# Mode products with the spectrum as the stationary operand and 512 weight columns moving

## Chip, cores, metric

One core of one Trainium2 chip. The metric is device microseconds (us) of one execution. "Before" and "after" are the kernel before and after the change. Medians stand with their ranges. With one core there is no second die to compare; the profiled runs and those in the ratios were judged fast. Times of different kernels are compared inside the same batch of rounds on the same chip. A trace is one profiled execution; its span is some 1.8 us shorter than the timed run, so traces are compared with traces.

## What is computed

Windowed attention (batch 8, 8 heads, 576 positions, head size 64), whose output `x` (8 x 576 x 512) goes into a spectral layer:

```python
X  = np.fft.rfft(x, axis=1)                       # along the sequence
Xr, Xi = X.real[:, :64], X.imag[:, :64]           # 64 modes are kept
Yr = einsum('bmd,mde->bme', Xr, w_r) - einsum('bmd,mde->bme', Xi, w_i)
Yi = einsum('bmd,mde->bme', Xr, w_i) + einsum('bmd,mde->bme', Xi, w_r)
y  = np.fft.irfft(Y, n=576, axis=1)               # Y is zero above mode 64
u  = x + y
return u + np.maximum(u @ w_ch, 0)
```

The weights `w_r` and `w_i` have 64 modes of 512 x 512 each. They are the bulk of what is read. Mode 0 has no imaginary part, so there are 127 products of one weight matrix with 16 rows (8 batches, real and imaginary).

## The kernel before

`XQ` holds the spectrum with contraction on the partitions: for each of four chunks `c` of the 512 channels, for each batch, three rows (-Xi, Xr, Xi) of 64 modes. A product of one weight is 16 small matmuls: a 128 x 128 block of the weight is loaded as the stationary operand and 16 columns of the spectrum move.

```python
def mode(m, between=lambda: None):
    wr, wi = wtiles.pop((m, 0)), wtiles.pop((m, 1), None)
    if m % MG == 0:
        psy = ps_y.tile([128, MG, NC, 2 * B], FP32, name="psy")
    for im, w in enumerate((wr, wi) if m else (wr,)):
        for e in range(NC):
            for c in range(NC):
                nc.tensor.matmul(out=psy[:, m % MG, e, :], lhsT=w[:, c, 128 * e:128 * e + 128],
                                 rhs=XQ[:, c, :, 1 - im:3 - im, m], ...)
        if im == 0:
            between()                 # other PE work: a turned spectrum
        refill_w(m, im)               # this weight's buffer is free: issue the next load into it
    if m % MG == MG - 1 or m == ME - 1:
        keep_y(m)                     # two copies from PSUM into YT
```

Weights come in through one queue, 512 KB a load, issued by POOL when a buffer comes free (`refill_w`):

```python
def load_w(i, pool, tag, wt=None):
    ...
    src = moe_w_i if im else moe_w_r
    nc.gpsimd.dma_start(out=wt, in_=src[m].rearrange("(p c) e -> p c e", c=NC))
```

The last four modes (60 to 63) have products of their own into `psl`, which the change leaves in their old form. Between them PE runs a filler, `idle`, whose results nothing reads:

```python
def idle(wide, n):
    ...                                # 'wide' matmuls of 512 columns, then
    for _ in range(10 * n):
        nc.tensor.matmul(out=psd[:, 0:48], lhsT=ident_bf, rhs=view(x_sb, 0, [[1, 48]]), ...)

for m in range(ME + 2, NM):            # modes 62 and 63
    for im in range(2):
        idle(1, 2)
        last(m, im)
idle(0, 2)
```

The softmax here doesn't subtract the row's maximum and nothing guards it: scores larger than these inputs give would overflow.

## Time and profile before

| | before |
|---|---|
| median of 3 runs | 428.31 us (428.12 to 428.38) |
| span of the trace | 426.7 us |
| instructions | 11631 |
| weight products | 127 x 16 matmuls, each with its weight load |

### The profile page before, as it was taken

What the parts mean: (1) busy time and instruction counts of PE and PEld (TensorE: products, weight loads), DVE (VectorE), ACT (ScalarE), POOL (GpSimd) and SP (SyncE); (2) the same over time, 40 slices, a digit from 0 to 9 for tenths busy, and PEclk for the clock granted to TensorE, in tenths of its full rate; (3) what the DMA queues carried; (4) which work ended last, traced back from release to release, by engine and by line L of the source; (5) the groups of instructions that cost most, each with busy time, mean ns of one, the idle gap of its engine ahead of it and who ended that gap; (6) DMA issues with size and microseconds to landing.
All of it is one profiled execution on the core that took longest, in us unless ns stands there. A gap on an engine that the chain in (4) does not pass through costs nothing.

```text
span 426.7 us, 11631 instructions
## 1 busy us (share of the span) xinstructions
PE 320.8 (75%) x5179; PEld 229.7 (54%) x5190; DVE 178.0 (42%) x375; ACT 165.0 (39%) x292; POOL 89.2 (21%) x171
## 2 busy tenths in 40 slices
PE   6989998999989865322497787887457685498993
PEld 5655765666665665321376666655244452265781
DVE  5566765766673200306333432221113432240994
ACT  4585766866773121001032322222113331130992
POOL 7231231331021321211121121121211122200000
PEclk9999999999995855555588998888558967589997
DMA  7999999999999999999999999999999999994598
GB/s 141 212 213 212 213 212 214 212 214 212 214 213 215 214 214 260 214 214 214 213 214 214 214 213 214 214 213 214 213 214 213 214 214 213 214 212 81 202 392 311
DMA packets 28657, 92.16 MB, mean 216 GB/s; under 512 B 2832, under 2 KB 3088, under 8 KB 28608
## 3 DMA queue, kind: packets, MB, share of 16 engines
q0 software_dynamic: 25344, 81.80, 96.2%
q1 hardware_dynamic: 3120, 9.50, 5.8%
q8 instruction: 40, 0.66, 0.6%
q10 hardware_dynamic: 144, 0.13, 0.1%
q14 instruction: 9, 0.07, 0.0%
HBM read 162.53 MB, written 9.44 MB: 403 GB/s over the span
## 4 chain that ended last, share of the span: by engine, by line
DMA 49%; PE 36%; DVE 8%; issue 4%; ACT 2%; POOL 1%; DVEq 0%; POOLq 0%
DMA wt<-in_moe_w_i_dram 22%; DMA wt<-in_moe_w_r_dram 18%; DMA wy<-in_moe_w_r_dram 9%; PE pso L316 7%; PE pst L218 6%; PE pso L870 4%; PE psv L235 3%; PE psy L563 3%; DVE x_sb L324 3%; PE pss L372 3%; PE pss L272 2%; PE psx L338 2%; PE pss L291 2%; DVE vT L59 2%; PE psz L596 1%
## 5 line engine op out<-in xcount | busy, mean ns | idle before, releaser
L563 PE MATMUL psy<-XQ,wt 128*128 128x16 bf16 x1616 | 61.3, 191 | 73.7 <-DMA wt<-in_moe_w_i_dram 34.7
L563 PEld LDWEIGHTS <-wt 128*128 128x128 bf16 x1616 | 53.0, 103 | 89.6 <-DMA wt<-in_moe_w_i_dram 39.7
L591 DVE CAST xT<-pxt 128x256 fp32r<-128x256 bf16 (+1 forms) x68 | 26.1, 434 | 61.6 <-PE pxt L584 39.7
L598 ACT CAST Z<-psz 128x512 fp32r<-128x512 f32 x36 | 21.1, 586 | 67.5 <-PE psz L596 67.5
L115 POOL DMA_DIRECT2D wt<-in_moe_w_r_dram x54 | 28.9, 536 | 87.3 <-DMA wt<-in_moe_w_r_dram 42.1
L596 PE MATMUL psz<-wch,xT 128*128 128x512 f32 x144 | 46.3, 465 | 0.0
L115 POOL DMA_DIRECT2D wt<-in_moe_w_i_dram x52 | 27.8, 535 | 85.7 <-DMA wt<-in_moe_w_i_dram 49.1
L297 ACT ACTIVATE et<-pss 128x512 bf16<-128x512 f32 x72 | 39.2, 600 | 13.4 <-PE pss L291 13.4
L316 PE MATMUL pso<-vt,et 128*64 128x65 bf16 (+1 forms) x576 | 34.3, 210 | 4.8 <-DVE x_sb L324 4.7
L316 PEld LDWEIGHTS <-et 128*64 128x64 bf16 (+1 forms) x576 | 24.0, 114 | 17.1 <-issue 9.6
L596 PEld LDWEIGHTS psz<-wch,xT 128*128 128x128 f32 x144 | 29.4, 218 | 5.9 <-ACT Z L598 0.3
L324 DVE TENSOR_TENSOR x_sb<-pso,rcp 128x640 bf16<-128x640 f32 x32 | 26.3, 823 | 0.9
L59 DVE CAST x_sb<-psj 128x512 bf16<-128x512 f32 x18 | 12.3, 689 | 26.3 <-PE psj L773 23.4
L870 PE MATMUL pso<-Y,trigI 128*128 128x512 f32 x80 | 23.1, 402 | 0.1
L893 DVE TENSOR_TENSOR ot<-pso,x_sb 128x512 f32<-128x512 f32 x35 | 22.2, 685 | 1.5 <-PE pso L870 1.1
L272 PE MATMUL pss<-band,ident_bf 64*64 64x512 bf16 x136 | 20.7, 414 | 1.5 <-ACT et L297 1.5
L58 ACT CAST YT<-psy 128x256 fp32r<-128x256 f32 x6 | 2.2, 372 | 50.6 <-DVE YT L59 50.6
L59 DVE COPY vT<-pst 128x768 bf16<-128x768 bf16 x16 | 15.3, 958 | 13.0 <-PE pst L218 13.0
L58 ACT CAST x_sb<-psj 128x512 bf16<-128x512 f32 x18 | 10.5, 585 | 25.7 <-PE psj L773 25.7
L59 DVE CAST YT<-psy 128x256 fp32r<-128x256 f32 x6 | 2.5, 425 | 42.9 <-PE psy L563 42.9
L875 ACT ACTIVATE pso<-pso 128x512 f32<-128x512 f32 x36 | 19.2, 596 | 0.0
L870 PEld LDWEIGHTS pso<-Y,trigI 128*128 128x128 f32 x80 | 14.5, 188 | 5.5 <-ACT pso L875 1.7
(160 smaller groups left out, 492.7 us busy)
## 6 DMA issues: line engine op xcount, KB each, us to landing
wt<-in_moe_w_r_dram POOLq DMA_DIRECT2D x54, 512.0 KB, 19.1
wt<-in_moe_w_i_dram POOLq DMA_DIRECT2D x52, 512.0 KB, 19.1
out_dram<-ot SPq DMA_DIRECT2D x15, 512.0 KB, 4.4
rk<-in_k_dram POOLq DMA_DIRECT2D x8, 576.0 KB, 9.8
rq<-in_q_dram POOLq DMA_DIRECT2D x8, 576.0 KB, 13.7
rv<-in_v_dram POOLq DMA_DIRECT2D x8, 576.0 KB, 12.4
wy<-in_moe_w_r_dram POOLq DMA_DIRECT2D x3, 512.0 KB, 17.0
wy<-in_moe_w_i_dram POOLq DMA_DIRECT2D x3, 512.0 KB, 19.1
```

The lines of the kernel that those rows point to most:

```text
L59: return nc.vector.tensor_copy(out=o, in_=i)
L115: nc.gpsimd.dma_start(out=wt, in_=src[m].rearrange("(p c) e -> p c e", c=NC))
L218: nc.tensor.transpose(out=ps[64 * hh:64 * hh + 64, c, :], in_=src[:, hh, (c0 + c) * D:(c0 + c + 1) * D], identity=ident_bf)
L272: nc.tensor.matmul(out=pss[(2 * w + hh) % 3][64 * half:64 * half + 64, :], lhsT=ident_bf[pp, pp], rhs=view(band[pp], 128 * half, [[0, WIN ...
L297: nc.scalar.activation(out=et[:, hh, :], in_=pss[(2 * w + hh) % 3], func=ACT_F.Exp, scale=EX_SCALE)
L316: nc.tensor.matmul(out=pso[po, hh, (i // 2) * VW:(i // 2) * VW + D + 1], lhsT=et[pk, hh, col:col + 64], rhs=vt[pk, 1 - f % 2, 2 * hh + g / ...
L324: nc.vector.tensor_tensor(out=view(x_sb, b * NT * DM + g * D, [[4 * D, 2], [DM, NT], [1, D]]), in0=view(pso, 0, [[512, 2], [VW, NT], [1, D]]),
L563: nc.tensor.matmul(out=psy[:, m % MG, e, :], lhsT=w[:, c, 128 * e:128 * e + 128], rhs=XQ[:, c, :, 1 - im:3 - im, m], start=(m % MG == im + ...
L591: nc.vector.tensor_copy(out=xT[:, :, w * k:w * k + w], in_=view(psts[k], j, [[128, NC], [n, w]] if n > 1 else [[128, NC], [1, 64], [64, 2]]))
L596: nc.tensor.matmul(out=psz, lhsT=xT[:, c, :], rhs=wch[:, c, :], start=(c == 0), stop=(c == NC - 1))
L870: nc.tensor.matmul(out=tps[n], lhsT=trigI[:, tr:tr + 128], rhs=pair_tile(what, bb), start=False, stop=stop and r0 + k == 128, skip_group_c ...
L893: nc.vector.tensor_tensor(out=ot[:, j], in0=ps, in1=x_sb[:, b, t, :], op=ALU.add)
```

## The change

Its intent: let the small operand (32 columns of spectrum) be stationary and the large one (512 weight columns) move, so that one weight costs 4 matmuls and 4 narrow loads in place of 16 and 16. The output then has 16 useful rows and 512 columns, so four modes share one PSUM tile of 128 x 512 as four blocks of 32 rows, and the result has to be turned by transposes every four modes. The spectrum is laid out with modes contiguous so that the 32 stationary columns have one stride.

```diff
-    XQ = xqp.tile([128, NC, B, 3, NM], BF16, name="XQ")
+    XQ = xqp.tile([128, NC, 3, B, NM], BF16, name="XQ")
 ...
-    def keep_y(m):
-        ... (two copies of psy into YT)
+    MQ = 4
+    held = []
+    def keep_y(m, ps):
+        half = [x_sb[:, 4 * (m // MQ % 2) + 1 + 2 * h, NT - 1, :].bitcast(FP32) for h in range(2)]
+        for h in range(2):
+            evac(half[h], ps[:, 256 * h:256 * h + 256], h)
+        def turn_rows():
+            psa = ps_a.tile([128, NC, 128], FP32, name="psa", tag="psa")
+            for e in range(NC):
+                nc.tensor.transpose(out=psa[:, e, :], in_=half[e // 2][:, 128 * (e % 2):128 * (e % 2) + 128], ...)
+            ... (two copies of psa into YT)
+        held.append(turn_rows)
 ...
     def mode(m, between=lambda: None):
-        if m % MG == 0:
-            psy = ps_y.tile([128, MG, NC, 2 * B], FP32, name="psy")
+        if m % MQ == 0:
+            psy = ps_y.tile([128, DM], FP32, name="psy")
+        r0 = 32 * (m % MQ)
         for im, w in enumerate((wr, wi) if m else (wr,)):
-            for e in range(NC):
-                for c in range(NC):
-                    nc.tensor.matmul(out=psy[:, m % MG, e, :], lhsT=w[:, c, 128 * e:128 * e + 128],
-                                     rhs=XQ[:, c, :, 1 - im:3 - im, m], ...)
+            for c in range(NC):
+                k = 32 if c < NC - 1 else 2 * B
+                nc.tensor.matmul(out=psy[r0:r0 + k, :], lhsT=xq(c, m, im, [[NM, k]]), rhs=w[:, c, :], ...)
             if im == 0:
+                while held:
+                    held.pop(0)()
                 between()
 ...
-        for _ in range(10 * n):
-            nc.tensor.matmul(out=psd[:, 0:48], ..., rhs=view(x_sb, 0, [[1, 48]]), ...)
+        for _ in range(5 * n):
+            nc.tensor.matmul(out=psd[:, 0:96], ..., rhs=view(x_sb, 0, [[1, 96]]), ...)
```

Cut: the indexing helper `xq`, the two copies that write the new layout of `XQ`, one copy moved from mode 8 to mode 1, and a last `held` call before the end.

More of the change, by code (lines that the diff above doesn't have):

```diff
@@ L347, in dft_turn @@
                                 identity=ident_bf)
-        BN = B * 3 * NM
-        nc.vector.tensor_copy(out=view(XQ, b * 3 * NM + NM, [[BN, NC], [1, 2 * NM]]), in_=ps.rearrange("p c r m -> p c (r m)"))
-        nc.scalar.mul(out=view(XQ, b * 3 * NM, [[BN, NC], [1, NM]]), in_=ps[:, :, 1, :], mul=-1.0)
+        nc.vector.tensor_copy(out=view(XQ, (B + b) * NM, [[3 * B * NM, NC], [B * NM, 2], [1, NM]]), in_=ps)
+        nc.scalar.mul(out=view(XQ, b * NM, [[3 * B * NM, NC], [1, NM]]), in_=ps[:, :, 1, :], mul=-1.0)
     nw = 0
@@ L540, in refill_w, with xq @@
             nw += 1
-    def rows_of(tile_, n, g, im, m0, nm):
-        return view(tile_, g * 2 * MG + im * nm + m0, [[B * n, NC], [n, B], [1, nm]])
-    def keep_y(m):
-        g = m // MG
-        n = MG if m < M0 + MG else ML
-        dst, k, g = (YT, E0, g) if g < L0 else (YTl, R, g - L0)
-        for ri in range(2):
-            evac(rows_of(dst, k, g, ri, 0, n),
-                 view(psy, ri, [[2 * B, NC], [2, B], [NC * 2 * B, n]]), ri)
+    MQ = 4
[7 more added lines that the diff above has]
+            for e in range(NC):
+                nc.tensor.transpose(out=psa[:, e, :], in_=half[e // 2][:, 128 * (e % 2):128 * (e % 2) + 128],
+                                    identity=ident_r.bitcast(FP32))
+            g = m // MG
+            n = MG if m < M0 + MG else ML
+            dst, k, g = (YT, E0, g) if g < L0 else (YTl, R, g - L0)
+            for ri in range(2):
+                evac(view(dst, g * 2 * MG + ri * n + m % MG - MQ + 1, [[B * k, NC], [k, B], [1, MQ]]),
+                     view(psa, B * ri, [[128, NC], [1, B], [32, MQ]]), ri)
+        held.append(turn_rows)
+    def xq(c, m, im, dims):
+        return view(XQ, (c * 3 + 1 - im) * B * NM + m, dims)
     def mode(m, between=lambda: None):
@@ L557, in mode @@
         wr, wi = wtiles.pop((m, 0)), wtiles.pop((m, 1), None)
-        if m % MG == 0:
-            psy = ps_y.tile([128, MG, NC, 2 * B], FP32, name="psy")
+        if m % MQ == 0:
+            psy = ps_y.tile([128, DM], FP32, name="psy")
+        r0 = 32 * (m % MQ)
         for im, w in enumerate((wr, wi) if m else (wr,)):
-            for e in range(NC):
-                for c in range(NC):
-                    nc.tensor.matmul(out=psy[:, m % MG, e, :], lhsT=w[:, c, 128 * e:128 * e + 128],
-                                     rhs=XQ[:, c, :, 1 - im:3 - im, m], start=(m % MG == im + e + c == 0),
-                                     stop=(im == (m > 0) and c == NC - 1), skip_group_check=True)
+            for c in range(NC):
+                k = 32 if c < NC - 1 else 2 * B
+                nc.tensor.matmul(out=psy[r0:r0 + k, :], lhsT=xq(c, m, im, [[NM, k]]), rhs=w[:, c, :],
+                                 start=(im + c == 0), stop=(im == (m > 0) and c == NC - 1), skip_group_check=True)
             if im == 0:
+                while held:
+                    held.pop(0)()
                 between()
             refill_w(m, im)
-        if m % MG == MG - 1 or m == ME - 1:
-            keep_y(m)
+        if m % MQ == MQ - 1:
+            keep_y(m, psy)
     with ExitStack() as p2a:
@@ L604 @@
             mode(m)
-            if m == 8:
+            if m == 1:
                 for b in range(1, B, 2):
@@ L726, in idle @@
             nc.tensor.matmul(out=psd, lhsT=ident_r.bitcast(FP32), rhs=Z0[:, 0, :].bitcast(FP32), start=True, stop=True)
-        for _ in range(10 * n):
-            nc.tensor.matmul(out=psd[:, 0:48], lhsT=ident_bf, rhs=view(x_sb, 0, [[1, 48]]), start=True, stop=True)
+        for _ in range(5 * n):
+            nc.tensor.matmul(out=psd[:, 0:96], lhsT=ident_bf, rhs=view(x_sb, 0, [[1, 96]]), start=True, stop=True)
     seq = []
@@ L763, in last_mode @@
                                  lhsT=w[:, c, 128 * e:128 * e + 128],
-                                 rhs=XQ[:, c, :, 1 - im:3 - im, m], start=(m == ME and im + c + e == 0),
+                                 rhs=xq(c, m, im, [[NM, B], [B * NM, 2]]), start=(m == ME and im + c + e == 0),
                                  stop=(im == 1 and c == NC - 1), skip_group_check=True)
@@ L803 @@
                 refill_w(m, 1)
+        while held:
+            held.pop(0)()
         NR = 2 * R + RL * (B - 2)
```

## The prediction

> **What bounds the kernel now.** I read the page first, then the chain of waits in order of time, then stretches of the span, then PE's timeline inside them. On the page, the clock, DMA and GB/s rows and the chain:
>
> ```profile
> PEclk9999999999995855555588998888558967589997
> DMA  7999999999999999999999999999999999994598
> GB/s 141 212 213 212 213 212 214 212 214 212 214 213 215 214 214 260 214 214 214 213 214 214 214 213 214 214 213 214 213 214 213 214 214 213 214 212 81 202 392 311
> DMA 49%; PE 36%; DVE 8%; issue 4%; ACT 2%; POOL 1%; DVEq 0%; POOLq 0%
> DMA wt<-in_moe_w_i_dram 22%; DMA wt<-in_moe_w_r_dram 18%; DMA wy<-in_moe_w_r_dram 9%; PE pso L316 7%; PE pst L218 6%; PE pso L870 4%; PE psv L235 3%; PE psy L563 3%; DVE x_sb L324 3%; PE pss L372 3%; PE pss L272 2%; PE psx L338 2%; PE pss L291 2%; DVE vT L59 2%; PE psz L596 1%
> ```
>
> From the second slice to the 36th (about 10 to 385 us) DMA stays at nine tenths and 212 to 214 GB/s, attention or no attention. The program is one stream of loads with compute hung on it. The end of that stream in the chain:
>
> ```profile
> 352.06 17.01 DMA wy<-in_moe_w_r_dram
> 369.60 19.99 DMA wy<-in_moe_w_r_dram
> 389.64 0.63 PE psl L762 x16
> 390.26 0.94 PE psd L726 x2
> 391.21 0.50 PE psd L728 x20
> 391.70 0.49 PE psl L762 x16
> ```
>
> So about 389.6 us is set by the transfers and 37 us of inverse transform follow. A change between 145 and 389 us matters only if it opens a gap in the stream or makes PE late at 389.6. PE there, by stretches (start and end, length, PE, PEld, DVE, ACT, POOL busy, clock, DMA share, GB/s):
>
> ```profile
> 148.58:172.00 23.42, 15.28 (x511) 14.74 (x507) 1.18 (x5) 4.19 (x7) 5.83 (x13) 0.50 1.09 235
> 173.00:210.00 37.00, 9.59 (x240) 8.00 (x240) 12.81 (x54) 2.81 (x11) 7.95 (x15) 0.50 1.06 213
> 211.00:297.00 86.00, 70.92 (x834) 54.32 (x830) 25.55 (x66) 21.48 (x38) 18.52 (x35) 0.88 1.06 214
> 313.00:372.00 59.00, 39.25 (x511) 25.18 (x511) 17.13 (x26) 14.46 (x26) 12.69 (x24) 0.73 1.06 214
> ```
>
> First PE works off the 29 or so weights that lie ready when the spectrum is done (145.6), then waits for each load, then shares its time with the channel products (psz), then with the turned spectra and the spreading of x. The operations to price, in PE's timeline (start, busy):
>
> ```profile
> 180.32 0.67 PE L563 MATMUL psy<-XQ,wt 128*128 128x16 bf16 x16 [1.83 <-DMA wt<-in_moe_w_r_dram]
> 241.06 2.12 PE L596 MATMUL psz<-wch,xT 128*128 128x512 f32 x8
> 322.94 0.62 PE L773 MATMUL psj<-x_sb,ident_bf 128*64 128x512 bf16 x4
> 357.33 1.06 PE L773 MATMUL psj<-x_sb,ident_bf 128*64 128x512 bf16 x4
> ```
>
> Sixteen small products of one weight cost 0.67 us, about 30 ns apart once streaming. Weights come every 2.45 us (PE's starts from 186.09 to 210.62: ten gaps). PE waits 1.83 of that.
>
> [...]eight psz in 2.12 us warm are 264 ns with their weight loads; four psj, two at a time, 0.62 warm and 1.06 cold[...]clock flips lie on a grid of 3.413 us (128.1, 141.8, 148.6, 216.9). [...]the psj pairs (64 output rows each, two column halves, different data) do run concurrently here.[...]
>
> **The change, part by part.**
> (1) Products. 119 weights (modes 0 to 59) go from 16 matmuls and 16 full weight loads to 4 matmuls of 512 columns with 32-column loads: 1428 matmuls and 1428 loads less. Time rises: from 0.48 us streaming to 4 x 0.216 = 0.87 us warm or 4 x 0.427 = 1.71 us cold. The last product of a mode and the first of the next are in different column tiles and may overlap: at best 7/8 of that. So PE gets 119 x 0.4 = 47 us more work warm, 119 x 1.2 = 145 us cold. All beside the stream as long as PE keeps up.
> (2) Turning. Every four modes: two copies of half a bank (0.42 and 0.37 us, the 128x256 rows of the YT copies), four 128x128 transposes (0.4 to 0.63 us, as psa now), two copies of 128 elements a row (0.29 and 0.27). About 1.4 us more latency and 0.5 us of PE for each of 15 groups: 0.06 us a weight.
> (3) Spectrum layout: same copies, other strides: nothing.
> (4) The idle filler: 10 matmuls of 96 columns (43 ns) for 20 of 48 (0.50 us in the chain): about -0.1 us each, twice after the last weight: -0.2 us.
> (5) Fetching: some 2700 of 11631 instructions go; the page gives instruction fetch 0.6% of the DMA span, so at most 0.23 x 0.6% x 427 = -0.6 us of the stream.
>
> **Does the stream get a gap?** 33 loads precede the products. By the refill rules load 34 and its four followers wait for modes 0 to 2, later ones for modes 3 to 14, and load 47 takes the buffer of weight 34. Now 47 goes out at 173.5 and lands some 19.1 later, at 192.6[...]. Warm, weight 34 is done at 145.6 + 34 x 0.9 = 176: no gap[...]. Later there are 13 buffers in rotation, 32 us of stream, so PE may lag over 25 us.
>
> **Warm or cold?** I summed in each 3.41 us window the columns moved, times contraction rows/128, concurrent column halves once[...]. [...]So narrow stationary operands should not count against the clock, and 512-column products back to back give 0.5 cold and 1.0 warm: PE stays warm from 145.6 through the backlog. In the pure waiting stretch they give [...]0.35: cold, 1.7 + 0.2 of every 2.45 us, still in time. From 211 to 297: per mode (4.9 us) 2 x 0.87 + 2.05 tiles x 1.35 (psz 1.06, transposes 0.3) = 4.5 us warm: tight, with the 25 us of slack behind it. From 313: 1.75 + one spectrum (1.14 + 0.41) + 1.67 spreads x 0.62 = 4.3 of 4.9, then four modes without a spectrum to catch up in.
>
> **The end.** After mode 59 the middle rows start at 372.8 now; (2) makes that 1.5 to 2 us later, a slower last product another 0.5. PE's waits from there to 389.6 are 0.52 + 0.21 + 0.34 + 0.39 + 1.28 = 2.7 us, so little comes through: +0.5. Sum: 428.3 - 0.2 - 0.5 + 0.5 = 428.1.
>
> **Rivals.**
> A: [...]Nothing in before has under 64 output columns, so my rule is extended beyond its data. Then PE goes cold at 148.6: weight 34 done at 148.6 + 30 x 1.7 = 200[...], and PE, 145 us heavier, becomes the bound in the last two stretches: 440 to 455. I give it 12%.
> B: PE warm but full between 211 and 372, kept from its order by copies on DVE and ACT (psj waits 0.8 us for its copies already), lags by more than the last four modes give back: 430 to 436.
> C: the gain meant by 1428 fewer loads arrives. For it: PEld is 54% busy. Against: all of it lies where PE waits for DMA. It would need the tail to shrink, which runs at full clock already: 425 at best.
>
> **Range and chances.** Most weight on 427 to 430, a tail upward from A and B. Range 426.8 to 436. Faster by over 2% (below 419.7): 0.03. Slower by over 2% (above 436.9): 0.14. Within: 0.83.
>
> **What will show it.** Right: GB/s still 212 to 214 to slice 36; the last product near 389.6; products of one weight about 0.9 us at clock 1.0 after 148.6; PE busier from 173 to 372. Wrong: clock 0.50 with dense products after 148.6; GB/s below 205 between 185 and 210; the psl products no longer waiting for DMA before 389; or a tail (last product to end) other than 35 us.

The figures for matmuls are also in the traces: 512 columns start 427 ns apart at half clock (psz in before) and 215 to 216 at full clock (psy in after), 96 columns 42 to 43 (the filler of after). Shares of a window are of the some 8100 columns that 3.41 us hold at 215 to 216 ns for 512. Rival A supposes that stationary columns count against the clock, of which there are only 32 of 128 after the change.

## More of the kernel before

From the page of the kernel before: the engines' busy time, the instruction queue q8 (packets, MB, share of the 16 DMA engines' time), which I take for PE's, and the two groups of the products (count, then busy us and mean ns of one, then idle time before them with its main cause).

```profile
PE 320.8 (75%) x5179; PEld 229.7 (54%) x5190; DVE 178.0 (42%) x375; ACT 165.0 (39%) x292; POOL 89.2 (21%) x171
q8 instruction: 40, 0.66, 0.6%
L563 PE MATMUL psy<-XQ,wt 128*128 128x16 bf16 x1616 | 61.3, 191 | 73.7 <-DMA wt<-in_moe_w_i_dram 34.7
L563 PEld LDWEIGHTS <-wt 128*128 128x128 bf16 x1616 | 53.0, 103 | 89.6 <-DMA wt<-in_moe_w_i_dram 39.7
```

PE is busy three quarters of the time, but its products wait 34.7 us for one kind of load alone.

0.66 MB over 40 packets is 16 KB a packet, and 10369 PE instructions over 40 packets are 259 to one (after: 7534 over 29, 260). Between the start of one packet and the next PE starts 255 instructions on average, in both traces.

## The result

| | before | after |
|---|---|---|
| median | 428.35 us (428.12 to 428.72, 4 runs) | 426.69 us (426.62 to 426.80, 4 runs) |
| ratio of fast runs | | 0.9961 (0.9943 to 0.9978) |
| span of the trace | 426.7 | 424.8 |
| last load landed (trace) | 391.42 | 390.00 |

The change is 0.4% faster: within 2% as predicted, but 1.4 us below the predicted 428.1 and 0.1 us below the low end of the range.

The page of the kernel after, the lines that answer to those of before:

```profile
span 424.8 us, 8859 instructions
PE 360.5 (85%) x3762; PEld 219.2 (52%) x3772; DVE 184.7 (43%) x397; ACT 171.4 (40%) x314; POOL 89.5 (21%) x171
PEclk9999999999995699965799998999999999999998
GB/s 144 212 213 212 213 213 212 213 213 213 213 214 213 215 213 261 213 214 213 214 213 214 213 214 214 213 215 212 214 213 213 214 213 215 213 214 95 195 384 329
q8 instruction: 29, 0.48, 0.4%
DMA 45%; PE 40%; DVE 8%; issue 2%; ACT 2%; POOL 1%; DVEq 0%; POOLq 0%
L575 PE MATMUL psy<-wt,XQ 128*32 128x512 bf16 (+1 forms) x404 | 96.6, 409 | 30.8 <-DMA wt<-in_moe_w_i_dram 15.5
```

The number of PE instructions fell by more than a quarter, PE's busy time rose by 40 us, and the stream of loads did not notice: from the second slice to the 36th 212 to 215 GB/s as before (but for the 16th, 261 for 260). The same four stretches as in the prediction (start and end, length, PE, PEld, DVE, ACT, POOL busy, clock, DMA share, GB/s):

```profile
148.58:172.00 23.42, 20.92 (x162) 13.82 (x160) 3.00 (x9) 3.65 (x11) 8.10 (x17) 1.00 1.08 235
173.00:210.00 37.00, 23.98 (x70) 8.20 (x69) 14.62 (x67) 4.99 (x15) 8.00 (x16) 0.72 1.06 213
211.00:297.00 86.00, 80.18 (x430) 49.32 (x430) 27.29 (x73) 22.78 (x44) 17.98 (x34) 0.97 1.06 213
313.00:372.00 59.00, 45.68 (x229) 22.86 (x231) 17.81 (x29) 15.60 (x30) 12.69 (x24) 0.99 1.06 213
```

PE is warm where the prediction said it would be (1.00 for 0.50 in the first stretch), and fuller everywhere. So the gain is not in these stretches. It is at the end of the stream. The end in the chain of waits of after (start, us, what):

```profile
370.83 19.17 DMA wy<-in_moe_w_i_dram
390.00 0.05 issue
390.05 0.67 PE psl L775 x16
```

and the last two products in PE's timeline, of the kernel before and then of after (the bracket is the wait ahead of it):

```profile
389.64 0.63 PE L762 MATMUL psl<-XQ,wy 128*128 128x16 bf16 x16 [1.28 <-DMA wy<-in_moe_w_r_dram]
391.55 0.64 PE L762 MATMUL psl<-XQ,wy 128*128 128x16 bf16 x16
```

```profile
387.55 0.65 PE L775 MATMUL psl<-XQ,wy 128*128 128x16 bf16 x16 [0.25 <-DMA wy<-in_moe_w_r_dram]
390.05 0.65 PE L775 MATMUL psl<-XQ,wy 128*128 128x16 bf16 x16 [0.48 <-DMA wy<-in_moe_w_i_dram]
```

After, PE waits for both loads and starts 0.05 us behind the last one. The last product comes 1.50 us earlier (390.05 for 391.55), the load under it 1.42 us earlier. From the start of the last product to the end of the span it is 34.8 us after and 35.1 before.

Why does the same number of bytes at the same rate land earlier? The traces have 16 completion marks for each load. I read them as one from each of the 16 DMA engines that the page counts; no mark has an engine's name. The marks of the last load, from the trace, in us:

```
before 385.40 385.45 385.61 385.63 385.69 386.07 386.18 387.03 | 389.94 390.97 391.02 391.09 391.10 391.15 391.17 391.42
after  385.27 385.35 385.36 385.38 385.55 385.84 386.15 386.81 | 388.40 388.51 388.85 388.97 389.84 389.90 389.91 390.00
```

Eight engines are done at about the same time in both kernels. The other eight are late, by up to 6.0 us before and 4.7 after, and the program waits for the latest. The spread grew over the run, in steps: in before it was 0.3 us at the first loads, 1.3 after the first fetched block of PE instructions, 2.4 after the 9th, 3.5 after the 17th, 4.6 after the 25th and 5.7 after the 33rd. Between these steps each block set one more mark back. The sixteen marks of three loads of before, in us from the first of the load (worked out from the trace):

```
3 blocks fetched   0.0 0.1 0.1 0.1 0.1 0.1 0.2 0.2 0.3 0.3 0.3 0.3 0.4 1.3 1.4 1.4
8                  0.0 0.1 0.2 0.2 0.3 0.4 0.5 0.6 1.1 1.1 1.2 1.3 1.3 1.3 1.3 1.3
9                  0.0 0.0 0.1 0.2 0.2 0.3 0.4 0.6 1.2 1.2 1.2 1.2 1.3 1.3 1.3 2.4
```

The duration of the fetch packets also repeats with a period of eight (893, 893, 949, 945, 936, 975, 974, 961 ns, and again from the start, in both kernels, with a few longer ones). From this and the steps of the spread I take it that PE's instruction fetches go round eight of the sixteen DMA engines, one 16 KB block each, and that a block sets its engine back by about 1.1 us (five steps from 0.3 to 5.7). Which engines they are the trace does not say. Blocks fetched more than 3 us before the last load was complete: 39 before (five on the fullest engine), 28 after (four). The marks of the last load above agree: 28 is three rounds of eight and four blocks, and of the late marks of after four lie at 388.40 to 388.97 and four at 389.84 to 390.00; 39 is four rounds and seven, and of those of before one lies at 389.94 and seven at 390.97 to 391.42.

There was one more thing in the trace of before that the prediction passed over. In the catch-up after 147 us PE waits for nothing that the profile shows ("issue"). First PE's waits, then its timeline:

```profile
PE psy L563 <- issue: 8.0, 4, 2.4
```

```profile
151.48 3.88 PE L563 MATMUL psy<-XQ,wt 128*128 128x16 bf16 x128 [1.38 <-issue]
157.40 0.50 PE L563 MATMUL psy<-XQ,wt 128*128 128x16 bf16 x11 [2.05 <-issue]
```

128 matmuls and their 128 loads are 256 instructions, which is what one packet brings by the counts above (255 to 260); they run 3.9 us and then PE stands for 2.05. The fetch packets started at 149.0, 155.1, 161.3, 167.2 and 173.2, some 6.0 us apart. I read this as PE being out of instructions: a block came each 6.0 us and lasted 3.9. What holds the fetch for so long is not shown (its packet takes 0.9 us). After the change there is no such wait. It cost the kernel before nothing: the stream stayed at 212 GB/s or more there (150 to 170 us).

### The profile page after: what moved, and what is told of

Its sections match the earlier page's. It is cut to its first block, busy times and chain, and to the rows that moved or that the text cites. A ratio compares the mean times of both kernels' runs of the same rounds, so it can differ in the third digit from the quotient of the medians.

```text
span 424.8 us, 8859 instructions
## 1 busy us (share of the span) xinstructions
PE 360.5 (85%) x3762; PEld 219.2 (52%) x3772; DVE 184.7 (43%) x397; ACT 171.4 (40%) x314; POOL 89.5 (21%) x171
## 4 chain that ended last, share of the span: by engine, by line
DMA 45%; PE 40%; DVE 8%; issue 2%; ACT 2%; POOL 1%; DVEq 0%; POOLq 0%
DMA wt<-in_moe_w_r_dram 32%; DMA wt<-in_moe_w_i_dram 9%; PE pso L316 7%; PE psy L575 7%; PE pst L218 6%; DMA wy<-in_moe_w_i_dram 5%; PE pso L885 4%; PE psv L235 3%; DVE x_sb L324 3%; PE psx L338 3%; PE pss L371 3%; PE pss L272 2%; PE pss L291 2%; DVE vT L59 2%; PE psw L724 1%
## 5 line engine op out<-in xcount | busy, mean ns | idle before, releaser
L575 PE MATMUL psy<-wt,XQ 128*32 128x512 bf16 (+1 forms) x404 | 96.6, 409 | 30.8 <-DMA wt<-in_moe_w_i_dram 15.5
L575 PEld LDWEIGHTS <-XQ 128*32 128x32 bf16 x476 | 48.6, 131 | 76.5 <-issue 57.0
L609 PE MATMUL psz<-wch,xT 128*128 128x512 f32 x144 | 42.4, 432 | 0.9 <-DVE xT L604 0.9
L609 PEld LDWEIGHTS psz<-wch,xT 128*128 128x128 f32 x144 | 27.1, 200 | 15.0 <-issue 8.7
L59 DVE COPY x_sb<-psy 128x256 f32<-128x256 f32 x15 | 6.4, 424 | 56.7 <-PE psy L575 56.7
L58 ACT COPY x_sb<-psy 128x256 f32<-128x256 f32 x15 | 5.6, 373 | 50.2 <-DVE x_sb L59 50.2
L291 PE MATMUL pss<-qT,kT 64*64 64x128 bf16 (+1 forms) x640 | 17.3, 221 | 0.3 <-issue 0.3
## 6 DMA issues: line engine op xcount, KB each, us to landing
wt<-in_moe_w_r_dram POOLq DMA_DIRECT2D x54, 512.0 KB, 19.1
wt<-in_moe_w_i_dram POOLq DMA_DIRECT2D x52, 512.0 KB, 19.1
wy<-in_moe_w_i_dram POOLq DMA_DIRECT2D x3, 512.0 KB, 19.1
```

Of the source, the lines that this page charges most:

```text
L59: return nc.vector.tensor_copy(out=o, in_=i)
L291: nc.tensor.matmul(out=pss[(2 * w + hh) % 3][64 * half:64 * half + 64, col:col + nq], lhsT=kTs[b % 2][pp, g, 64 * kb:64 * kb + 64], rhs=qT ...
L575: nc.tensor.matmul(out=psy[r0:r0 + k, :], lhsT=xq(c, m, im, [[NM, k]]), rhs=w[:, c, :], start=(im + c == 0), stop=(im == (m > 0) and c == ...
L609: nc.tensor.matmul(out=psz, lhsT=xT[:, c, :], rhs=wch[:, c, :], start=(c == 0), stop=(c == NC - 1))
```

## The experiments

**Theory F:** the gain is that fewer blocks are fetched, and it comes in whole blocks on the fullest of eight DMA engines. **Rival L:** fetching costs in proportion to the number of instructions. **Rival E:** the end of the program got faster by the other filler or by an earlier start of PE. The expectations also name a rival C: the gain comes from the form of the products (warmer clock, buffers free earlier).

### The changed kernel with its products cut into columns

Four matmuls of 128 columns in place of one of 512; the same with two of 256. All data, buffers and results stay, only the number of PE instructions grows.

```diff
+                for n0 in range(0, DM, DM // p):          # p = 4, or 2
+                    cols = slice(n0, n0 + DM // p)
-                nc.tensor.matmul(out=psy[r0:r0 + k, :], ..., rhs=w[:, c, :], start=(im + c == 0), ...)
+                    nc.tensor.matmul(out=psy[r0:r0 + k, cols], ..., rhs=w[:, c, cols], start=(im + c + n0 == 0), ...)
```

> The changed kernel with each mode product of 512 columns cut into four of 128: same layout, same array time (4 x 53 ns for 213), but about 2860 more PE instructions, which brings their number back to that of before. Theory F (fetch: every block of 256 PE instructions, 16 KB, holds one of eight DMA engines for about 1.1 us, and the stream ends with the engine that had most): some 11 blocks more, 39 before the end of the stream, five on an engine for four: the last load lands 1.1 to 1.4 us later, 427.8 to 428.4 us, equal to before. Rival C (the gain comes from the form of the product: warmer clock, earlier release of buffers): stays at 426.7, at most 0.3 above. Rival E (shorter filler and end of PE's list): stays at 426.7.

Measured: 429.23 us (428.7 to 429.63), ratio 1.0011 (0.9997 to 1.0026); before in the same rounds 428.45. Last load at 391.31, with 39 blocks ahead of it, as in the kernel before. The array time is the same: from 147.29 us 128 products of 128 columns took 6.82 us, 53 ns each, and one of 512 takes 215 in the changed kernel.

> The same with two pieces of 256 columns: about 950 more PE instructions, 3.7 blocks, so 32 at most before the end of the stream. Theory F with whole blocks per engine: still four on the fullest engine, last landing within 0.3 us of the changed kernel's 390.0, 426.6 to 427.1 us. A linear version of F (bytes spread over eight engines, 0.14 us a block): +0.5, about 427.2. Rivals C and E: 426.7.

Measured: 426.86 us (426.57 to 429.08), ratio 0.9967 (0.9947 to 0.9987). Last load at 389.88, with 32 blocks ahead of it.

The structure of the change with the instruction count of before has the landing of before, so the whole gain goes with the instructions (against E and C). And four more blocks (28 to 32) cost nothing, eleven cost 1.3 us (for F, against L). The quarters are a further 0.8 us worse than F's range; two parts of that are in the trace. PE starts the last product 0.43 us behind its load (391.74), and a fetch fell at 417.4, among the output stores; the tail from the last product to the end was 35.6 us.

### The changed kernel with the old filler

```diff
-        for _ in range(5 * n):
-            ... rhs=view(x_sb, 0, [[1, 96]])
+        for _ in range(10 * n):
+            ... rhs=view(x_sb, 0, [[1, 48]])
```

> The changed kernel with the old filler (20 matmuls of 48 columns for 10 of 96). Prediction on record: the new filler saves 0.1 us each, one after the last landing counts: 426.7 + 0.1. Theory F: 100 instructions more are 0.4 of a block: nothing, so 426.7 to 426.9. Rival E (the shorter filler made the gain): 427.5 or more.

Measured: 427.11 us (426.87 to 427.63), ratio 0.9963 (0.9948 to 0.9978). Last load 390.07, last product 390.12, so the stream's end has not moved. The median lies 0.2 us above F's range and well under E's 427.5. The tail is 35.7 us for 34.8, with a fetch at 409.2, among the stores.

### The kernel before with the new filler

> The kernel before with the new filler alone (half as many matmuls, of 96 columns for 48): some 100 matmuls and as many weight loads less, under one fetch block. My prediction gave this part -0.2 us. Theory F: 38 or 39 blocks, still five on the fullest engine, last landing 391.3 to 391.5, and PE waits for the last load in place of being late by some 0.1: 428.1 to 428.4, ratio 0.999 to 1.000. Rival E (the gain of the change lies in the filler, not in the stream): 426.7 to 427.2.

Measured: 428.27 us (428.04 to 428.37), ratio 0.9995 (0.9982 to 1.0007); before 428.38. Last load 391.51, last product 391.55. The filler is worth 0.1 us, not the gain.

### The kernel before with 8-column products

```diff
+                    for h in range(2):
-                        ... out=psy[:, m % MG, e, :], rhs=XQ[:, c, :, 1 - im:3 - im, m]
+                        ... out=psy[:, m % MG, e, B * h:B * h + B], rhs=XQ[:, c, B // 2 * h:B // 2 * h + B // 2, 1 - im:3 - im, m]
```

> The kernel before with every product of 16 columns cut into two of 8: about 3810 more PE instructions, 15 blocks, 54 before the end of the stream, seven on the fullest engine for five. Theory F: last landing 2 to 2.6 us later, 430.3 to 431.0 us. Rivals C and E: PE has room for it (about 0.5 us more per weight, it waits 1.8 us for each), so 428.3 to 428.6.

Measured: 436.23 us (434.5 to 438.26), ratio 1.0176 (1.0151 to 1.0201). Far more than expected, and for another reason. The page's GB/s row, then PE's waits (us in total, times, longest), then lines of PE's timeline:

```profile
GB/s 143 212 214 211 214 213 212 213 213 214 213 215 213 215 213 261 205 89 211 213 213 214 214 214 213 215 213 212 216 213 214 214 213 214 213 213 106 182 394 315
```

```profile
PE psy L564 <- issue: 22.9, 11, 2.9
```

```profile
181.40 0.46 PE L564 MATMUL psy<-XQ,vT 128*128 128x8 bf16 x11 [2.34 <-issue]
187.60 0.47 PE L564 MATMUL psy<-XQ,vt 128*128 128x8 bf16 x11 [2.61 <-issue]
201.25 3.58 PE L564 MATMUL psy<-XQ,wt 128*128 128x8 bf16 x128 [2.34 <-issue]
```

The 18th slice (about 184 to 195 us) falls to 89 GB/s. PE now needs 64 instructions a weight, so a block of 256 lasts four weights; at a block each 6.0 us that is 1.5 us a weight, whatever the matmuls take. Weight 34, whose buffer a later load needs, would be done at 147 + 35 x 1.5 = 199.5 (my estimate from these numbers). In the kernel before that later load (47) goes out at 173.5 and, with the median of 19.1 us, lands near 192.6. POOL issued the next loads only at 188.4 and 192.9, and the last load landed 7.3 us late. So here, if the waits on "issue" are waits for instructions, the fetches are the bound through PE, not through the stream's end. This run does not separate F from L.

### The step between 32 and 39 blocks

```diff
+                p = 4 if m % 3 == 1 else 2        # parts of the columns, as in the first experiment
```

> The changed kernel with its products in two or four column parts, so that some 34 or 35 blocks of PE instructions are fetched before the last load has landed (28 in the changed kernel, 32 with halves, 39 with quarters and in the kernel before). Theory F (whole blocks: the fetches rotate over 8 of the 16 DMA engines, about 1.1 us each, and the stream ends with the fullest of them): with 33 to 40 blocks the fullest engine has five, as with 39, so the last load lands at 391.2 to 391.5 in the trace and the time is 427.8 to 428.6, no different from the kernel before. Rival L (the fetches cost in proportion to their number, as in my prediction but larger): last landing 390.4 to 390.7, time 427.2 to 427.6.

Measured: 428.7 us (428.25 to 429.12), ratio 1.001 (0.9997 to 1.0023); before in these rounds 428.3. 34 blocks ahead of the last load, which landed at 391.02; PE started 0.04 us behind it. A fetch at 415.5 fell among the stores and the tail was 35.7 us.

Two more blocks than the halves, 1.14 us later; L would give a quarter of that. The marks show the two: with halves (32 blocks, four rounds of eight) all eight late marks of the last load lie at 389.72 to 389.88; here (four rounds and two) six lie at 389.75 to 390.33 and two at 390.91 and 391.02. The landing is 0.2 us under F's range. The time is 0.1 us over it, from the tail.

### More blocks in the kernel before, where PE has time

```diff
+                    p = 2 if m in range(45, 57) else 1      # two products of 8 columns in 12 modes
```

> The kernel before, with the 16-column products of modes 45 to 56 alone cut into two of 8 columns: 768 more PE instructions, three fetch blocks, in a stretch where PE waits for loads anyway (313 to 372 us). Theory F (whole blocks over 8 of 16 DMA engines): 42 blocks in place of 39 before the last load, so the fullest engine has six, the last load lands at 392.3 to 392.7 in the trace (391.4 before), time 429.2 to 429.8, or up to 0.8 more if a fetch falls among the output stores after 405 us, ratio 1.002 to 1.004; PE starts the last two products of the load stream no later after their loads than before, and GB/s stays at 212 to 214 to slice 36. Rival L (in proportion to the number of blocks, some 0.13 us each from 1.42 us for 11): last load at 391.8, time 428.8. Rival P (the split kernel of the first batch was slow by work on PE alone, not by fetching): no change of the landing, 428.4, or a gap in GB/s.

Measured: 429.07 us (428.92 to 429.18), ratio 1.0013 (1.0000 to 1.0027); before 428.38. 42 blocks, last load at 392.07, no gap in GB/s, and PE waits for the last product:

```profile
392.12 0.65 PE L767 MATMUL psl<-XQ,wy 128*128 128x16 bf16 x16 [0.34 <-DMA wy<-in_moe_w_i_dram]
```

The landing moved by 0.65 us, between F (0.9 or more) and L (0.4). P is excluded: PE was early and the stream was full. So instructions alone move the end of the stream, in the kernel before too. The size of the sixth block was smaller than F said.

### Can the late engines be relieved?

The fourth load from the end was issued in pieces, in the hope that they fall on some of the engines only: first seven DMAs of 17 partitions and one of 9, then DMAs of 8 partitions, large and small by turns. On which engines such pieces fall is not shown, and what the three expectations assumed of it is cut from them; their forecasts rested on that.

```diff
-        nc.gpsimd.dma_start(out=wt, in_=rows)
+        step = 17 if i == NLOAD - 4 else 128
+        for p in range(0, 128, step):
+            nc.gpsimd.dma_start(out=wt[p:min(p + step, 128)], in_=rows[p:min(p + step, 128)])
```

> The changed kernel, with the fourth load from the end (512 KB) issued as seven DMAs of 17 partitions and one of 9. [...]Theory F says that 8 engines are some 3.5 us later than the other 8 at the end of the stream: if the late ones are the high half, the last load lands 1 to 2 us earlier (388 to 389 in the trace) and the spread of its 16 landing marks shrinks from 4.7 to about 1 or 2 us, time 424.7 to 425.7; if the late ones are the low half, the spread grows to about 9 us and the last load lands at 392 to 393, time 428.5 to 429.5. If each small DMA falls on one engine or on all, no clear sign; the spread of the marks will say. Rival: no pattern by engine, the lag is one of the queue as a whole: spread and time as in the changed kernel, 426.7.

Measured: 428.8 us (428.19 to 429.14), ratio 1.001 (0.9995 to 1.0026). POOL's timeline shows what happened: each small DMA waited for the landing of an earlier load, and the last three loads were issued 11 to 15 us later than in the changed kernel.

```profile
377.81 0.50 POOL L118 DMA_DIRECT2D wt<-in_moe_w_r_dram  x1 [1.98 <-DMA wt<-in_moe_w_r_dram]
380.46 0.50 POOL L118 DMA_DIRECT2D wt<-in_moe_w_r_dram  x1 [2.15 <-DMA wt<-in_moe_w_r_dram]
380.97 0.54 POOL L118 DMA_DIRECT2D wy<-in_moe_w_i_dram  x1
382.18 0.53 POOL L118 DMA_DIRECT2D wy<-in_moe_w_i_dram  x1
```

The queue ran dry (149 GB/s in the 36th slice, 214 in the changed kernel), and the last load landed at 391.89, with a spread of only 1.3 us: fifteen marks within 0.3 us and one 1.0 behind them. The queue had been empty, and one block of instructions (380.4) was fetched about then, so one late engine is what F expects. As a cure it failed, and the time says nothing about F. The marks of the small DMAs say a little: with each of them eight marks moved on by about 0.6 us, one by 0.3, the others by 0.2. So by the marks the pieces did not load all engines alike. Of the eight that moved most six were early engines and two were late ones: this split would have loaded two of the late ones further.

> The changed kernel, with the fourth load from the end issued as 25 DMAs of 8 partitions, by turns large (four row chunks) and small (one), the large one first. [...]Theory F: the spread of the landing marks of the last load goes from 4.7 us to under 2.5 or to over 6, opposite in this run and the next, and the time by 1 us or more to the same side, that is 425 to 425.8 or 427.7 to 428.5. [...]Risk in both: 25 issues on POOL take over 13 us in place of 0.5 and may open a gap in the stream, seen as GB/s below 200 before 385.

> As the run before, with the small DMA first[...]. Theory F: whatever the run with the large one first does to the spread of the last load's landing marks and to the time, this one does the opposite.

Measured: 436.08 (435.81 to 436.24) and 435.96 us (435.79 to 436.05), ratios 1.0182 and 1.0179, alike. This is the risk that was named: GB/s fell to 37 in the 36th slice in the first of them. In its POOL timeline the first eight of the 25 issues come 2.2 to 2.7 us apart (363.34 to 380.52), each held until an earlier load has landed, and the last three loads are issued at 389.36 to 390.43, for 380.97 to 382.18 with eight pieces. They tell nothing on F.

### All landings together

| kernel | blocks before the last load | last load landed | last product | tail to the end | a fetch after 405 us |
|---|---|---|---|---|---|
| after | 28 | 390.00 | 390.05 | 34.8 | no |
| after, old filler | 28 | 390.07 | 390.12 | 35.7 | yes |
| after, halves | 32 | 389.88 | 389.94 | 34.8 | no |
| after, halves and quarters | 34 | 391.02 | 391.06 | 35.7 | yes |
| after, quarters | 39 | 391.31 | 391.74 | 35.6 | yes |
| before | 39 | 391.42 | 391.55 | 35.1 | no |
| before, new filler | 39 | 391.51 | 391.55 | 34.9 | no |
| before, 12 modes split | 42 | 392.07 | 392.12 | 35.3 | no |

Four blocks on the fullest engine (25 to 32): 389.9 to 390.1. Five (33 to 40): 391.0 to 391.5. Six: 392.1. A straight line through the first and last rows (0.15 us a block) would put 32 blocks at 390.6, where 389.88 was measured, and 34 at 390.9. I take the step as shown between 32 and 34. Between single traces the fifth block costs 0.9 to 1.6 us and the sixth 0.6 to 1.1. Why the sixth is smaller stays open.

The tails differ in the stores alone: in all eight kernels PE is done 27.9 to 28.0 us after the start of the last product and DVE 29.2 to 29.3, but the last packet of the stores ends at 34.2 with such a fetch and at 33.2 to 33.8 without. This was seen, not tested by itself.

No version beat the changed kernel. By this count (an estimate) the next step down would need 24 blocks or fewer ahead of the last load, four less than it has, and 20 of its 28 are fetched by 151.3 us, in the part that the change does not touch.

## Why the prediction was off

By its own steps:

1. **Products warm, no gap, PE in time: right.** Clock 1.00 from 148.6, the four matmuls of a weight 215 ns apart (0.9 us predicted for the four), GB/s unchanged, and PE busy 35.7 us longer over the four stretches (170.8 for 135.0) without any effect on the stream. Rival A (stationary columns count against the clock) is refuted by the 1.00 with 32 of 128 columns stationary; rival B did not come. Three readings were off and cost nothing. In the backlog the second weight of a mode ran beside the first of the next, two weights in 0.93 us (157.51 to 158.44), so 0.47 each, where the prediction allowed 7/8 of 0.87 at best. The waiting stretch (173 to 210 us) was forecast cold, at 0.35 of a window on average, but 0.72 of the clock was granted. A sharp boundary of the clock by columns moved is not shown: counted by the starts of the matmuls, with products of 64 output columns taken as half, the 34 half-clock windows (3.41 us each) of before that were followed by half clock hold up to 0.41, the ten followed by full clock 0.30 to 0.48, and in after the one at 370.4 us had 0.25 and was followed by full clock. And the first load of the trace took 5.6 us from issue to landing, 1.5 of them to its first packet. With that on an empty queue (an estimate) load 47 could go out as late as 192.6 - 5.6 = 187.0, and weight 34, done at 176 in the prediction, had 11 us to spare.
2. **Turning:** the chain of waits passes over some of it (0.60 us of transposes at 314.87), but the stream has no gap, so none of it delays the end.
3. **Filler, -0.2 us:** measured -0.1 on the kernel before (428.27 for 428.38). Right in size, small either way.
4. **Fetching, "at most 0.23 x 0.6% x 427 = -0.6 us of the stream": this is the term that failed.** The mechanism was named and its sign was right. Its size was 1.42 us in the trace. The step averaged the packet time over 16 engines and so called the average a maximum; and it took the share of all instructions that go, 0.23, where the queue of PE alone lost 11 of 40 blocks. The fetches fall on eight engines in blocks of 16 KB, and the stream ends with the fullest of them: five blocks against four. Eight engines for 16 and 11/40 for 0.23 would have made the term 1.4 us; the whole blocks decide what the neighbours (32 and 34 blocks) cost.
5. **The end, "+0.5":** measured 0. PE waited 0.25 and 0.48 us for the last two loads although these came earlier, so what PE lost between 372 and 387 us was made up in its waits entirely. The prediction itself had counted 2.7 us of waits there and should have let them absorb the half microsecond.

Put in: 428.35 - 0.1 - 1.4 + 0 = 426.85, against 426.69 measured. The prediction's rival C (fewer weight loads, seen in a shorter tail, 425 at best) did not come: the tail is 0.3 us shorter in one trace against one trace, and the kernel before with the new filler shows 0.2 of that without the change. Fewer weight loads did pay, but as instructions that need not be fetched.

## What to carry to other kernels

In this kernel, which is bound by a stream of loads, the row of the instruction queue belonged to the bill: 0.6 and 0.4% of the DMA time on the page, and 1.42 us at the end of the stream between 39 and 28 blocks. To make the same bill elsewhere, count the PE instructions by the block (256 here), find how many engines the blocks go round (eight here) and take the fullest engine, not the average over sixteen; then see whether a change crosses a step (0.9 to 1.6 us here from four blocks to five). The sixteen landing marks of a load show it directly. And where PE stands in a run of tiny matmuls on "issue" after each 128 of them with their 128 loads, it may be waiting for its program: here fewer and larger matmuls took those 8.0 us of waits away.
